# Attention and two MLPs in one kernel: scales packed with q and k, V loaded earlier, weight decodes held in program order

## The chip, the core and the metric

One core of a Trainium2 chip runs the kernel. TensorE multiplies matrices (PE in the rows; PEld is its loading of weights), VectorE (DVE) and ScalarE (ACT) work elementwise and can read TensorE's accumulators in PSUM, GpSimd (POOL) works elementwise on SBUF, and SyncE (SP) issues the DMAs between main memory and SBUF. Each engine takes its instructions in the order of its own list and waits on semaphores for the others. The metric is the device time of one execution in microseconds (us); less is better.

## The reference

Windowed attention over 4 sequences of 576 positions with 8 heads of 64, then a gated MLP, then a bilinear one. Everything is float32, apart from weights that arrive as 64-bit floats.

```python
scores = q @ k.T / 8 + slope[h] * -abs(i - j)   # masked outside 0 <= i - j < 128
x = softmax(scores) @ v                         # 2304 x 512 when heads are joined
h = x @ w_in                                    # 512 -> 2048
x = (s * relu(h) ** 2 + b) @ w_out              # 2048 -> 512
out = (((x @ w1) * (x @ w2)) @ w3) @ w_out2     # 512 -> 1024 -> 1024 -> 512
```

## The kernel before

The 2304 tokens go in six tiles of 384. Attention works by head: head number g counts through the tiles, 0 to 7 are tile 0's, 8 to 15 tile 1's. Tile 0's heads go as four pairs, in plain float32; from head 8 on operands are split into a high and a low part. A head has these steps: the scores `s` (TensorE, lines 292 or 297 and 298), the minimum with the bias `ns` (VectorE, line 311), a fold `pr` (VectorE, 320), the exponential (ScalarE, 328 or 334), the norm `sm` (VectorE, 344 and 345) and its product (GpSimd, 347), transposes `te` or `tp` (TensorE, 361 or 368), copies `oe` or `pp`, the masks `pt` (GpSimd, 384), and the product with V, `xo` or `pv` (TensorE, 401 or 421). For tile 0 a pair's result is divided by its sums on VectorE (`rs`, lines 433 and 436, and `xs`, 438), transposed (443) and copied by ScalarE to `xe` (461). Pairs are numbered 0 to 3. The four `xe` tiles are the input of tile 0's first MLP.

That MLP goes in 16 chunks of 128 hidden units, in plain float32: `hp` (TensorE, line 482) needs all four `xe` and one chunk of `w_in`; ScalarE takes relu and square; `acc` (534) needs them and one chunk of `w_out`. Later tiles use lines 491 and 540, three passes over split operands.

The 32 weight chunks arrive as 64-bit floats (`raw`), and each is **decoded** once: ScalarE reads the upper words (line 98, `z`), VectorE shifts (100), puts the sign in (103) and joins the lower words (109, `wz`). From tile 1 on a chunk must also be **split** into two parts: ScalarE makes the first (131), GpSimd or VectorE in turn the second (132). All chunks, decoded, raw and split, share one pool of 33 buffers, so that a split finds a free buffer only when the one before it, or the last decode, has given one back.

The program is written as `slot`s. Eight slots do tile 0's heads, with decodes ticked in between; then ten slots, in the order "BBBABBABBB", do one head of the next tile each, and in those with a B also two chunks of tile 0's MLP, with two decodes in the middle of the slot and one at its end. From the eighth MLP slot on, each does four splits. The order of the lists is not the written one: a list scheduler with its own idea of durations places each instruction on its engine when it thinks that the engine and the inputs are free, and so moves a ready instruction ahead of others. `keep_in_program_order` holds one instruction behind the instruction that was written just before it for the same engine:

```python
        if prev is not None:
            self.add_manual_dep(ins.ins, prev.name, ...)
```

Of the kernel before, what the change touches and what calls it, by code (L numbers as in the profile page):

```python
# [8 lines left out]
F32 = mybir.dt.float32  # L9
# [3 lines left out]
AF = mybir.ActivationFunctionType  # L13
ALU = mybir.AluOpType

B, H, S, D = 4, 8, 576, 64
# [5 lines left out]
P = 128  # L22
TT = 384
# [9 lines left out]
EARLY = H  # L33
# [4 lines left out]

@with_exitstack
def kernel(  # L40
    ctx: ExitStack, tc: tile.TileContext, qk0, qk, v, relm, w_in, w_out, s, b, w1, w2, w3T, wo2, qsc, v0, out
):
    nc = tc.nc
    PSUM = bass.MemoryType.PSUM

    const = ctx.enter_context(tc.tile_pool(name="const", bufs=1))
# [9 lines left out]
    ap = att_ctx.enter_context(tc.tile_pool(name="ap", bufs=1))  # L56

    zeros = ap.tile([P, DM], BF16, tag="xf", name="zeros")
    qsc_sb = const.tile([P, H // 2], F32, name="qsc_sb")
    relm_sb = const.tile([P, 4, 2 * P], F32, name="relm_sb")  # L60
    ident = const.tile([P, P], F32, name="ident")
    s_sb = const.tile([P, 1], F32, name="s_sb")
# [17 lines left out]
    def raw_load(dst, src):  # L80
        i = nc.sync.dma_start(out=dst, in_=src)
        if keep[0]:
            tc.keep_in_program_order(i)
        return dst

    def decode(raw, pool, tag, done, free=None, plain=False):

        z = zp.tile([P, DM], F32, tag="z", name="z")  # L90
        if raw.dtype == F32:
            nc.vector.tensor_copy(out=z, in_=raw)
            yield
        else:
            zu = z.bitcast(U32)
            wu = raw.bitcast(U32).rearrange("p (n t) -> p n t", t=2)
            wf = raw.bitcast(F32).rearrange("p (n t) -> p n t", t=2)
            nc.scalar.activation(out=z, in_=wf[:, :, 1], func=AF.Copy, scale=2.0 ** -112)
            yield
            nc.vector.tensor_scalar(  # L100
                out=zu, in0=zu, scalar1=3, scalar2=None, op0=ALU.logical_shift_left
            )
            nc.vector.scalar_tensor_tensor(  # L103
                out=zu, in0=wu[:, :, 1], scalar=0x80000000, in1=zu,
                op0=ALU.bitwise_and, op1=ALU.bitwise_or,
            )
            if plain:
                z = pool.tile([P, DM], F32, tag=tag, name="wz")
            nc.vector.scalar_tensor_tensor(
                out=z.bitcast(U32), in0=wu[:, :, 0], scalar=29, in1=zu,  # L110
                op0=ALU.logical_shift_right, op1=ALU.bitwise_or,
            )
            if plain:
                done(z)
                yield
                return
        if free:
            free()
        yield
        w = pool.tile([P, 2, DM], F32R, tag=tag, name="w")  # L120
        nc.scalar.activation(out=w[:, 0, :], in_=z, func=AF.Copy)
        nc.gpsimd.tensor_tensor(
            out=w[:, 1, :], in0=z, in1=w[:, 0, :].bitcast(F32), op=ALU.subtract
        )
        done(w)
        yield
# [53 lines left out]
    def pre_tick(more=True):  # L180
        for p in pres:
            if p[1] is None or next(p[1], p) is p:
                p[1] = None
                if more and npre[0] < len(late):
                    p[1] = predecode(npre[0], p[0])
                    npre[0] += 1
                    next(p[1])

    flight, todo, keep, raws, nraw, need = [], [], [True], [], [0], [0]

    def load_raws(n):
        for _ in range(n):
            if nraw[0] < len(raws):
                raw_load(*raws[nraw[0]])
                nraw[0] += 1
# [13 lines left out]
    qkraw, vraw, qa, ka, kb, vv, ns, pr, mins, sums, tps, pt, xf, xT, xo = ({} for _ in range(15))  # L209

    def att_load(g):
        if g < NG:
            if g < EARLY and g % 2:
                return
            raw = ap.tile([P, 2 * TT + P], F32, tag="qkraw", name="qkraw", bufs=2)
            nc.sync.dma_start(out=raw, in_=qk0[g // 2] if g < EARLY else qk[g - EARLY])
            if g < EARLY:
                qkraw[g + 1] = raw
            qkraw[g] = raw

    def att_load_v(g):
        if g < NG and g % 2 == 0:
            m = 2 * (D + 1) if g < EARLY else 2 * D
            raw = ap.tile([P, NB + 1, m], F32, tag="vraw", name="vraw", bufs=2)
            src = v0[g // 2] if g < EARLY else v[(g - EARLY) // 2]
            nc.sync.dma_start(out=raw.rearrange("p n d -> p (n d)"), in_=src)
            vraw[g // 2] = raw

    def att_split_q(g):
        if g < NG:  # L230
            sc = -0.125 * 2.0 ** (g % H + 1)
            q_r = qkraw[g][:, :TT]
            if g < EARLY:
                if g % 2 == 0:
                    p = g // 2
                    a = ap.tile([P, TT], F32, tag="qa", name="qe", bufs=2)
                    nc.scalar.activation(
                        out=a, in_=q_r, func=AF.Identity, scale=qsc_sb[:, p:p + 1]
                    )
                    qa[g] = qa[g + 1] = a  # L240
                return
            a = ap.tile([P, TT], F32R, tag="qa", name="qa", bufs=2)
            nc.scalar.activation(out=a, in_=q_r, func=AF.Copy, scale=sc)
            nc.vector.scalar_tensor_tensor(
                out=a[D:, :], in0=q_r[D:, :], scalar=sc, in1=a[D:, :].bitcast(F32),
                op0=ALU.mult, op1=ALU.subtract,
            )
            qa[g] = a

    def att_split_k(g):  # L250
        if g < NG:
            k_r = qkraw.pop(g)[:, TT:]
            if g < EARLY:
                ka[g] = k_r
                return
            k = ap.tile([P, TT + P], F32R, tag="ka", name="ka", bufs=2)
            kl = ap.tile([P, TT + P], F32R, tag="kb", name="kb", bufs=2)
            nc.scalar.activation(out=k, in_=k_r, func=AF.Copy)  # L258
            nc.gpsimd.tensor_tensor(  # L259
                out=kl, in0=k_r, in1=k.bitcast(F32), op=ALU.subtract  # L260
            )
            ka[g], kb[g] = k, kl
# [388 lines left out]
    for c in range(NC1):  # L651
        for d, src in ((wi, w_in[c]), (wo, w_out[c * P:(c + 1) * P, :])):
            raw = wp.tile([P, DM], src.dtype, tag="w", name="raw")
# [4 lines left out]
                )  # L658
            )
    att_load(0)  # L660
    warm = const.tile([P, 1], F32, name="warm")
    nc.gpsimd.memset(zeros, 0.0)
    nc.vector.memset(warm, 0.0)
    nc.scalar.activation(out=warm, in_=warm, func=AF.Exp)
    nc.sync.dma_start(out=qsc_sb, in_=qsc)
    nc.sync.dma_start(out=relm_sb[:, :2], in_=relm[:, :2])
    load_raws(4)
    att_load_v(0)
    att_load(2)
    nc.sync.dma_start(out=s_sb, in_=s)  # L670
    nc.sync.dma_start(out=b_sb, in_=b)
    make_identity(nc, ident)
# [90 lines left out]
        slot(n, None)  # L763
    flush(EARLY - 1)
    n, m = EARLY, 0
    for k in "BBBABBABBB":
        slot(n if k in "AB" else None, m if k in "MB" else None)
        n += k in "AB"
        m += k in "MB"
    assert (n, m) == (18, 8), (n, m)  # L770
    last = LEAD + (NTILE - 1) * NC1 // 2
    for n in range(n, last):
        if n == LEAD + NC1 - 1:
# [132 lines left out]
```

## Time and profile before

| what | us |
|---|---|
| median of three runs | 911.92 |
| lowest and highest of them | 906.9 and 913.98 |
| the profiled execution | 907.65 |
| its span, first to last instruction | 905.9 |
| TensorE busy in the span | 887.2 |
| VectorE, ScalarE, GpSimd busy | 484.6, 453.4, 340.4 |

The profiled execution lies 4.3 us under the median, within what the runs differ by. TensorE's busy time is that of its records, whose ends are modelled: where it is busy throughout with few instructions, it may still be waiting or running at half clock. So the table says where to look (TensorE), and a view by stretch of time says when it has too little to do.

### The profile page before, as it was taken

To read this page: it belongs to the slowest core of one execution; us is meant where nothing else is said; L and a number is where in the kernel's file an instruction comes from. 1 tells how busy PE (TensorE), PEld (TensorE's weight loads), DVE (VectorE), ACT (ScalarE), POOL (GpSimd) and SP (SyncE) were. 2 spreads that over 40 slices of the span, in tenths; PEclk is the share of its full clock that TensorE was granted. 3 is DMA by queue.
4 is the path that set the end of the run, shared out by engine and by line. 5 is a ranking of instruction groups with operands and counts; after the bars stand their busy time and mean duration, and the time that the engine had idled before them with its cause. 6 is when DMAs were issued, how large, how long until landed. Compare 5 with 4: busy or idle time off the path is not lost.

```text
span 905.9 us, 13384 instructions
## 1 busy us (share of the span) xinstructions
PE 887.2 (98%) x4833; PEld 805.5 (89%) x4836; DVE 484.6 (53%) x1012; ACT 453.4 (50%) x1052; POOL 340.4 (38%) x376
## 2 busy tenths in 40 slices
PE   8989989999999999999999999999999999999997
PEld 4756656999999999999999999899999999999996
DVE  5998866766688887788752621482211212121212
ACT  5756667776767787777754543342212121121211
POOL 0154687775567686777641301240101001010000
PEclk8989999999999999999999999999999999999999
DMA  8974211213334455445326962130201002000000
GB/s 312 304 283 166 100 64 46 85 59 112 99 127 166 169 201 170 145 157 181 117 94 224 385 261 84 56 116 1 71 1 35 36 1 70 1 36 1 35 1 36
DMA packets 37219, 104.38 MB, mean 115 GB/s; under 512 B 4512, under 2 KB 10656, under 8 KB 37152
## 3 DMA queue, kind: packets, MB, share of 16 engines
q1 hardware_dynamic: 37152, 103.52, 33.0%
q8 instruction: 38, 0.62, 0.3%
q14 instruction: 29, 0.24, 0.1%
HBM read 82.00 MB, written 21.50 MB: 114 GB/s over the span
## 4 chain that ended last, share of the span: by engine, by line
PE 85%; DVE 6%; issue 2%; POOL 2%; ACT 2%; DMA 2%; SPq 1%; DVEq 0%; ACTq 0%; POOLq 0%
PE ab L611 21%; PE acc L540 17%; PE hp L491 17%; PE acc L637 11%; PE hp L482 3%; PE acc L534 3%; PE pv L421 3%; PE w3a L575 2%; DVE z L103 2%; PE tp L368 1%; PE s L298 1%; PE s L297 1%; PE s L292 1%; DMA vraw<-v 1%; DVE z L100 1%
## 5 line engine op out<-in xcount | busy, mean ns | idle before, releaser
L611 PE MATMUL ab<-x,w 128*128 128x384 f32 x1152 | 208.3, 335 | 0.0
L611 PEld LDWEIGHTS ab<-x,w 128*128 128x128 f32 x1152 | 201.8, 188 | 4.3
L491 PE MATMUL hp<-x,w 128*128 128x384 f32 x960 | 186.2, 340 | 0.9 <-DVE pp L381 0.9
L540 PE MATMUL acc<-gh,w 128*128 128x384 f32 x640 | 177.3, 339 | 0.0
L491 PEld LDWEIGHTS hp<-x,w 128*128 128x128 f32 x960 | 167.6, 188 | 1.4 <-DVE pp L381 1.1
L625 DVE TENSOR_TENSOR a<-ab,a 128x384 f32<-128x384 f32 x48 | 26.7, 557 | 197.7 <-PE ab L611 179.8
L540 PEld LDWEIGHTS acc<-gh,w 128*128 128x128 f32 x640 | 115.3, 188 | 0.3
L540 PE MATMUL acc<-gl,w 128*128 128x384 f32 x320 | 108.6, 339 | 1.5 <-DVE gl L520 1.5
L599 POOL TENSOR_TENSOR x<-x,x 128x384 fp32r<-128x384 f32 x24 | 25.6, 1093 | 203.8 <-ACT x L598 191.9
L347 POOL TENSOR_SCALAR pr<-pr,sm 128x128 f32<-128x128 f32 x120 | 63.5, 543 | 88.3 <-DVE sm L345 34.7
L637 PE MATMUL acc<-w3o,ph 128*128 128x512 f32 x288 | 89.9, 394 | 0.0
L624 ACT ACTIVATE a<-ab 128x384 f32<-128x384 f32 x48 | 23.6, 492 | 131.7 <-PE ab L611 131.7
L259 POOL TENSOR_TENSOR kb<-qkraw,ka 128x512 fp32r<-128x512 f32 x40 | 56.2, 1404 | 71.4 <-ACT ka L258 71.3
L384 POOL TENSOR_SCALAR_AFFINE_SELECT pt<-pp 128x768 fp32r<-128x768 f32 x80 | 77.2, 986 | 7.0 <-PE pv L421 6.5
L520 DVE TENSOR_TENSOR gl<-r,gh 128x384 fp32r<-128x384 f32 x80 | 57.8, 723 | 33.6 <-ACT gh L512 32.4
L311 DVE CUSTOM_DVE_ANT_0 ns<-s,relm_sb 128x256 f32<-128x256 f32 (+1 forms) x144 | 52.9, 412 | 39.2 <-PE s L298 30.1
L626 ACT ACTIVATE ph<-a 128x384 fp32r<-128x384 f32 x48 | 25.2, 525 | 92.7 <-DVE a L625 92.7
L502 ACT ACTIVATE r<-hp 128x384 f32<-128x384 f32 x96 | 46.5, 486 | 49.6 <-PE hp L491 43.5
L540 PEld LDWEIGHTS acc<-gl,w 128*128 128x128 f32 x320 | 60.3, 188 | 2.3 <-DVE gl L520 2.2
L637 PEld LDWEIGHTS acc<-w3o,ph 128*128 128x128 f32 x288 | 53.4, 187 | 8.9
L637 PE MATMUL acc<-w3o,pl 128*128 128x512 f32 x144 | 56.5, 396 | 0.2 <-DVE pl L627 0.2
L334 ACT ACTIVATE pr<-pr,mn 128x128 f32<-128x128 f32 x120 | 46.8, 392 | 19.3 <-DVE pr L320 16.6
(89 smaller groups left out, 1423.4 us busy)
## 6 DMA issues: line engine op xcount, KB each, us to landing
qkraw<-qk SPq DMA_DIRECT2D x45, 448.0 KB, 3.3
late<-st SPq DMA_DIRECT2D x23, 512.0 KB, 3.4
w<-late SPq DMA_DIRECT2D x23, 512.0 KB, 7.1
raw<-w_in SPq DMA_DIRECT2D x16, 512.0 KB, 7.1
raw<-w_out SPq DMA_DIRECT2D x16, 512.0 KB, 6.7
raw<-w SPq DMA_DIRECT2D x16, 512.0 KB, 5.2
st<-w3T SPq DMA_DIRECT2D x15, 512.0 KB, 3.8
vraw<-v SPq DMA_DIRECT2D x20, 256.0 KB, 2.6
```

Of the source, the lines that this page charges most:

```text
L259: nc.gpsimd.tensor_tensor(out=kl, in0=k_r, in1=k.bitcast(F32), op=ALU.subtract)
L311: nc.vector.tensor_tensor_reduce(out=n[:, i, cs], in0=dst[i][:, cs], in1=relm_sb[:, VARIANT.get(t * NB + i, 0), cs], scale=2.0 ** -(h + 1) ...
L334: nc.scalar.activation(out=e[:, i, :], in_=e[:, i, :], func=AF.Exp, scale=-1.0, bias=mn[:, i:i + 1], accum_out=sm[:, i:i + 1],)
L347: nc.gpsimd.tensor_scalar(out=e[:, i, :], in0=e[:, i, :], scalar1=sm[:, i:i + 1], scalar2=1.0, op0=ALU.mult, op1=ALU.mult,)
L384: nc.gpsimd.affine_select(out=o[:, :, :, e, :], in_=pp.bitcast(F32), pattern=[[0, 2], [0, NB], [sign, P]], compare_op=op, fill=0.0, base=0 ...
L421: nc.tensor.matmul(out=d, lhsT=l, rhs=r, start=(n == 0), stop=(n == len(mms) - 1), skip_group_check=True)
L491: nc.tensor.matmul(out=hp, lhsT=wi[c][:, l, k * P:(k + 1) * P], rhs=xT[t, k][:, r, :], start=(n == 0), stop=(n == 3 * KD - 1),)
L502: nc.scalar.activation(out=rt[:, :TT], in_=hps.pop((t, c)), func=AF.Relu)
L520: nc.vector.tensor_tensor(out=gl, in0=rt[:, :TT], in1=gh.bitcast(F32), op=ALU.subtract)
L540: nc.tensor.matmul(out=x2acc[m], lhsT=wo[c][:, l, ms], rhs=g[r], start=(c == 0 and n == 0), stop=(c == NC1 - 1 and n == 2),)
L611: nc.tensor.matmul(out=d, lhsT=w[c][:, l, k * P:(k + 1) * P], rhs=x2[t, k][:, r, :], start=(n == 0), stop=(n == 3 * KD - 1),)
L637: nc.tensor.matmul(out=oacc[i], lhsT=p[l][:, cs], rhs=w3o[c][:, r, :], start=(c == 0 and n == 0), stop=(c == NC2 - 1 and n == 2),)
```

## The change

Three edits. The scale of each pair's q, which came by a DMA of its own (`qsc`, 16 bytes for each partition), is appended as a 897th column to the pair's q and k (`qk0`), and ScalarE reads it there. In the first loads, V of pair 0 now goes ahead of the weights, and the second pair's q and k stand after two weight chunks instead of four. In the ten slots of tile 0's MLP, three of a decode's four instructions (ScalarE's, and the first two of VectorE) are held in program order. Nothing else of the computation differs.

```diff
--- before.py
+++ after.py
@@ -38,7 +38,7 @@
-    ctx: ExitStack, tc: tile.TileContext, qk0, qk, v, relm, w_in, w_out, s, b, w1, w2, w3T, wo2, qsc, v0, out
+    ctx: ExitStack, tc: tile.TileContext, qk0, qk, v, relm, w_in, w_out, s, b, w1, w2, w3T, wo2, v0, out
...
-    qsc_sb = const.tile([P, H // 2], F32, name="qsc_sb")
...
@@ -88,6 +87,7 @@
         z = zp.tile([P, DM], F32, tag="z", name="z")
+        pin = tc.keep_in_program_order if pinned[0] else lambda i: i
...
@@ -95,15 +95,15 @@
-            nc.scalar.activation(out=z, in_=wf[:, :, 1], func=AF.Copy, scale=2.0 ** -112)
+            pin(nc.scalar.activation(out=z, in_=wf[:, :, 1], func=AF.Copy, scale=2.0 ** -112))
             yield
-            nc.vector.tensor_scalar(
+            pin(nc.vector.tensor_scalar(
                 out=zu, in0=zu, scalar1=3, scalar2=None, op0=ALU.logical_shift_left
-            )
-            nc.vector.scalar_tensor_tensor(
+            ))
+            pin(nc.vector.scalar_tensor_tensor(
                 out=zu, in0=wu[:, :, 1], scalar=0x80000000, in1=zu,
                 op0=ALU.bitwise_and, op1=ALU.bitwise_or,
-            )
+            ))
...
@@ -212,7 +213,8 @@
-            raw = ap.tile([P, 2 * TT + P], F32, tag="qkraw", name="qkraw", bufs=2)
+            n = 2 * TT + P + (1 if g < EARLY else 0)
+            raw = ap.tile([P, n], F32, tag="qkraw", name="qkraw", bufs=2)
...
@@ -232,10 +234,9 @@
-                        out=a, in_=q_r, func=AF.Identity, scale=qsc_sb[:, p:p + 1]
+                        out=a, in_=q_r, func=AF.Identity, scale=qkraw[g][:, -1:]
...
@@ -662,11 +663,11 @@
-    nc.sync.dma_start(out=qsc_sb, in_=qsc)
     nc.sync.dma_start(out=relm_sb[:, :2], in_=relm[:, :2])
-    load_raws(4)
     att_load_v(0)
+    load_raws(2)
     att_load(2)
+    load_raws(2)
...
@@ -763,11 +764,13 @@
     n, m = EARLY, 0
+    pinned[0] = True
     for k in "BBBABBABBB":
         slot(n if k in "AB" else None, m if k in "MB" else None)
         n += k in "AB"
         m += k in "MB"
     assert (n, m) == (18, 8), (n, m)
+    pinned[0] = False
```

The host side appends the scale to `qk0` and drops `qsc`.

How this moves the lists is shown at three places. SyncE's first issues before; `qkraw` is a pair's q and k, `relm` the bias table, `raw` a weight chunk, `vraw` a pair's V:

```order
L216 DMA qkraw<-qk 128x896
L665 DMA qsc_sb<-qsc 128x4
L666 DMA relm_sb<-relm 128x512
L81 DMA raw<-w_in 128x512
L81 DMA raw<-w_out 128x512
L81 DMA raw<-w_in 128x512
L81 DMA raw<-w_out 128x512
L226 DMA vraw<-v 128x520
L216 DMA qkraw<-qk 128x896
```

and with the change:

```order
L218 DMA qkraw<-qk 128x897
L666 DMA relm_sb<-relm 128x512
L228 DMA vraw<-v 128x520
L80 DMA raw<-w_in 128x512
L80 DMA raw<-w_out 128x512
L218 DMA qkraw<-qk 128x897
L80 DMA raw<-w_in 128x512
L80 DMA raw<-w_out 128x512
```

The small load is gone, V has moved from eighth to third, and the second pair's q and k from ninth to sixth.

VectorE's list before, from the sums of pair 3 (`rs`) to its output (`xs`); the rows of `z` and `wz` are decodes, those of `ns` the minimum of head 9:

```order
L433 TENSOR_SCALAR rs<-xo 128x6
L103 SCALAR_TENSOR_TENSOR z<-raw,z 128x512
L100 TENSOR_SCALAR z<-z 128x512
L436 RECIPROCAL rs<-rs 128x6
L109 SCALAR_TENSOR_TENSOR wz<-raw,z 128x512
L311 ISA ns,mn<-s_679,relm_sb 128x256
L311 ISA mn 128x1
L311 ISA ns,mn<-s_679,relm_sb 128x256
L311 ISA mn 128x1
L103 SCALAR_TENSOR_TENSOR z<-raw,z 128x512
L438 TENSOR_TENSOR xs<-xo,rs 128x384
```

and with the change, from pair 2's second `rs` row on; the first `xs` is pair 2's, the second pair 3's:

```order
L437 RECIPROCAL rs<-rs 128x6
L100 TENSOR_SCALAR z<-z 128x512
L439 TENSOR_TENSOR xs<-xo,rs 128x384
L103 SCALAR_TENSOR_TENSOR z<-raw,z 128x512
L245 SCALAR_TENSOR_TENSOR qa<-qkraw,qa 64x384
L109 SCALAR_TENSOR_TENSOR wz<-raw,z 128x512
L434 TENSOR_SCALAR rs<-xo 128x6
L437 RECIPROCAL rs<-rs 128x6
L439 TENSOR_TENSOR xs<-xo,rs 128x384
```

Pair 3's `rs`, reciprocal and `xs` now stand in one piece. Ahead of that `xs` VectorE has 12 whole decodes instead of 15, and the minima of heads 8 and 9, the fold of head 8 and head 9's `qa` have all moved behind it.

GpSimd's list before, around its first split (the row of `w`); the `pt` behind it is head 12's:

```order
L259 TENSOR_TENSOR kb<-qkraw,ka 128x512
L347 TENSOR_SCALAR pr<-pr,sm 128x128 x3
L132 TENSOR_TENSOR w<-wz,w 128x512
L384 AFFINE_SELECT pt<-pp 128x6x128 x2
L275 TENSOR_TENSOR vv<-vraw,vv 128x4x64 x2
L465 TENSOR_TENSOR x<-xf,x 128x384
```

and with the change, up to its first split; the `pt` ahead of it is head 15's:

```order
L276 TENSOR_TENSOR vv<-vraw,vv 128x4x64 x2
L466 TENSOR_TENSOR x<-xf,x 128x384
L260 TENSOR_TENSOR kb<-qkraw,ka 128x512
L348 TENSOR_SCALAR pr<-pr,sm 128x128 x3
L385 AFFINE_SELECT pt<-pp 128x6x128 x2
L132 TENSOR_TENSOR w<-wz,w 128x512
```

GpSimd's first split has moved behind three more heads. On ScalarE, 8 splits instead of 22 now stand ahead of the first relu of tile 1's MLP. TensorE's list keeps its order of stages; `hp` of chunks 3 and 4 moves behind `acc` of chunks 0 and 1. From head 24 on TensorE's list is the same.

## Rows read from the trace of the kernel before

**Rows 1.** Stretches: busy us (x count) of PE, PEld, DVE, ACT, POOL; PE clock; DMA.

```profile
0.00:36.00 36.00, 32.43 (x155) 20.79 (x157) 24.13 (x83) 23.25 (x51) 1.16 (x7) 0.91 0.86 295
...
40.00:61.00 21.00, 17.75 (x72) 11.16 (x72) 20.67 (x45) 13.58 (x37) 10.41 (x9) 0.84 0.86 311
...
61.00:90.00 29.00, 29.00 (x114) 18.61 (x112) 26.91 (x62) 17.50 (x40) 13.47 (x17) 1.00 0.55 193
...
90.00:110.00 20.00, 20.00 (x87) 13.42 (x86) 17.49 (x39) 12.56 (x33) 11.67 (x15) 1.00 0.33 113
...
110.00:126.00 16.00, 11.98 (x46) 7.58 (x46) 11.36 (x27) 10.69 (x29) 15.39 (x16) 0.89 0.13 46
...
126.00:160.00 34.00, 34.00 (x143) 22.75 (x142) 19.36 (x48) 24.42 (x57) 27.21 (x31) 1.00 0.18 57
```

**Rows 2.** The same view, where tile 1's MLP runs.

```profile
165.00:200.00 35.00, 35.00 (x219) 34.87 (x219) 22.49 (x51) 27.45 (x68) 25.15 (x30) 1.00 0.18 53
```

**Rows 3.** Timeline, 4 to 15 us: start, us, engine, line, out<-in, idle before and releaser.

```profile
4.34 0.61 ACT L237 ACTIVATE qe<-qkraw,qsc_sb 128x384 f32<-128x384 f32 x1 [2.04 <-DMA qsc_sb<-qsc]
...
8.24 0.66 ACT L98 ACTIVATE z<-raw 128x512 f32<-128x512 f32 x1 [3.29 <-DMA raw<-w_in]
...
12.85 1.96 PE L401 MATMUL xo<-vraw,oe 128*128 128x65 f32 x10 [1.32 <-DMA vraw<-v]
```

**Rows 4.** Timeline of VectorE: sums of pair 2, output of pair 3.

```profile
39.76 0.16 DVE L433 TENSOR_SCALAR rs<-xo 128x6 f32<-128x6 f32 x1
...
53.24 0.55 DVE L438 TENSOR_TENSOR xs<-xo,rs 128x384 f32<-128x384 f32 x1
```

**Rows 5.** The chain of waits: start, us, what.

```profile
54.98 4.21 PE hp L482 x6
...
110.27 1.24 POOL w L132
...
122.65 4.28 PE hp L482 x8
...
136.76 2.58 PE hp L482 x8
...
151.65 0.88 PE pv L421 x8
...
155.69 0.12 PE s L297
```

**Rows 6.** Timeline of TensorE, the last chunk of tile 0's MLP.

```profile
156.25 2.75 PE L534 MATMUL acc<-r,wz 128*128 128x386 f32 x8
```

**Rows 7.** VectorE's groups from 60 to 165 us: line, form, count, busy us, mean ns.

```profile
L109 DVE SCALAR_TENSOR_TENSOR wz<-raw,z 128x512 uint32<-128x512 uint32 x15 | 12.3, 820 | 0.1
...
L103 DVE SCALAR_TENSOR_TENSOR z<-raw,z 128x512 uint32<-128x512 uint32 x14 | 12.2, 875 | 0.2
...
L100 DVE TENSOR_SCALAR z<-z 128x512 uint32<-128x512 uint32 x14 | 6.7, 480 | 0.2
...
L311 DVE CUSTOM_DVE_ANT_0 ns<-s,relm_sb 128x256 f32<-128x256 f32 x27 | 10.1, 419 | 4.1 <-PE s L298 4.1
...
L244 DVE SCALAR_TENSOR_TENSOR qa<-qkraw,qa 64x384 fp32r<-64x384 f32 x9 | 9.5, 1055 | 0.8 <-ACT qa L243 0.5
...
L320 DVE TENSOR_TENSOR pr<-ns 128x384 f32<-128x384 f32 x9 | 7.2, 796 | 0.3
...
L344 DVE TENSOR_SCALAR sm<-sm 128x3 f32<-128x3 f32 x10 | 5.0, 498 | 1.3 <-ACT pr L334 1.3
...
L453 DVE TENSOR_TENSOR xf<-pv,cs 64x384 f32<-64x384 f32 x8 | 4.4, 549 | 3.7 <-ACT cs L452 3.7
...
L381 DVE TENSOR_TENSOR pp<-tp,pp 128x384 fp32r<-128x384 f32 x10 | 5.4, 545 | 2.2 <-ACT pp L380 2.2
```

**Rows 8.** VectorE's groups from 0 to 36 us.

```profile
L103 DVE SCALAR_TENSOR_TENSOR z<-raw,z 128x512 uint32<-128x512 uint32 x10 | 6.9, 687 | 0.1
```

**Rows 9.** Line 131, ScalarE's part of a weight's split: ns, first and last start.

```profile
L131 ACT ACTIVATE w<-wz x32: 612/630/636, 108.5 to 191.6; 128x512 fp32r<-128x512 f32 x32
```

More of the change, by code (lines that the diff above doesn't have):

```diff
@@ L187, in pre_tick @@
                     next(p[1])
+    pinned = [False]
     flight, todo, keep, raws, nraw, need = [], [], [True], [], [0], [0]
@@ L234, in att_split_q @@
                 if g % 2 == 0:
-                    p = g // 2
                     a = ap.tile([P, TT], F32, tag="qa", name="qe", bufs=2)
                     nc.scalar.activation(
-                        out=a, in_=q_r, func=AF.Identity, scale=qsc_sb[:, p:p + 1]
+                        out=a, in_=q_r, func=AF.Identity, scale=qkraw[g][:, -1:]
                     )
@@ L251, in att_split_k @@
         if g < NG:
-            k_r = qkraw.pop(g)[:, TT:]
+            k_r = qkraw.pop(g)[:, TT:2 * TT + P]
             if g < EARLY:
@@ L859 @@
         else:
-            qk0 = rows.reshape(H // 2, P, 2 * TT + P)
+            sc = (-0.125 * 2.0 ** (np.arange(H) + 1)).astype(np.float32)
+            sc = np.repeat(sc, D).reshape(H // 2, P, 1)
+            qk0 = np.concatenate([rows.reshape(H // 2, P, 2 * TT + P), sc], 2)
         vt.append(
@@ L889 @@
     arrays["wo2"] = inputs["moe2_w_out"]
-    sc = (-0.125 * 2.0 ** (np.arange(H) + 1)).astype(np.float32)
-    arrays["qsc"] = np.repeat(sc.reshape(H // 2, 2), D, 1).T
     arrays["v0"] = v0
```

## The prediction

> **What bounds the kernel now.** I read first the view by stretch, to see where TensorE has too little to do [rows 1]. From 61 to 110 us and from 126 to 160 it is busy throughout at the full clock of 2.4 GHz, and also where tile 1's MLP runs [rows 2]. Three stretches are left: the start (32.43 of 36 us busy), 40 to 61, and 110 to 126. The table says 887.2 busy of a span of 905.9, so nearly all that can be won without less work on TensorE lies ahead of 126 us, and an edit counts if it shortens one of these three or opens a new one.
>
> From 40 to 61 VectorE is busy 20.67 of 21 us [rows 1], TensorE 17.75. VectorE's timeline says why: pair 2's sums are worked on at 39.76, pair 3's output only at 53.24 [rows 4]; decodes and minima of heads 8 and 9 stand between them. The chain of waits shows what this holds: `hp` goes on at 54.98, in 4.21 us for six matmuls [rows 5], 0.70 each, where later eight take 2.58, 0.32 each. So TensorE waited, and just behind the wait runs at the lower clock, 1.2 GHz. The granted clock of that stretch, 0.84, gives 0.16 x 21 = 3.4 us lost to it.
>
> From 110 to 126 TensorE is busy 11.98 of 16 at a granted clock of 0.89 [rows 1]: 4.0 us idle and 0.11 x 16 = 1.8 to the clock. The chain of waits passes there through GpSimd's split at 110.27 (1.24 us), and `hp` at 122.65 takes 4.28 for eight [rows 5]: splits stand ahead of head 12's work on GpSimd, and the clock has fallen behind the wait again.
>
> **The start.** ScalarE's `qe` waits 2.04 us for the small load, and the first product with V waits 1.32 for V [rows 3]. Both look like gains. But the pair's q and k are in the same queue just ahead of the small load, so the wait changes its name; a small load's worth, some 0.2, is the most. V moved ahead puts the first weights later by its own size: 128 x 520 x 4 bytes = 266 KB at the stretch's 295 GB/s [rows 1] is 0.9 us. ScalarE's first decode row (8.24 us, waiting for its weight [rows 3]) stands ahead of head 0's exponentials, and what they hold is the copies that the same product needs beside V. So the 1.32 goes to that: at best 1.3 less, at worst 0.9 more. I take 0, since V and the weight trade places in one chain.
>
> **Pair 3's output.** In the new list VectorE has, behind pair 2's sums at 39.76 [rows 4], the reciprocal, one shift and pair 2's `xs`, all of them short: up to 41.0. Pair 2's transposes and heads 6 and 7's products follow on TensorE (20 records by 0.12 as `s` [rows 5] = 2.4, and hand-overs): 43.7. One half decode, one `qa` and one joining on VectorE lie beside these. Then pair 3's sums, reciprocal and `xs` in one piece, 45.2; and from `xs` to `hp` before took 54.98 - 53.24 = 1.74 [rows 4, 5], with the last of pair 3's products and hand-overs less: 46.5. So `hp` goes on 8.5 us earlier. TensorE's list has then done less: six matmuls of `hp` and the scores of head 9 are now behind, 6 x 0.32 + 6 x 0.12 = 2.7 us. Since the wait is short, I take the lower clock's 3.4 as won too. What is late next is `acc` of chunk 0: ScalarE has an exponential, two first steps of decodes (0.66 each [rows 3]), head 9's operands, relu and square ahead of it. I take 1.5, with 0 and 4 as ends.
>
> The sum goes by the end of tile 0's MLP, where TensorE's order is again the old one. It was 156.25 + 2.75 = 159.0 [rows 6]. From 54.98 that is 104.0, of which 3.4 + 4.0 + 1.8 were lost: 94.8 of work at full clock, with the 2.7 97.5. The new time without further waits is 46.5 + 1.5 + 97.5 = 145.5, **13.5 earlier**. In this the losses of 110 to 126 are taken as gone, because GpSimd's first split stands behind three more heads in the new list, as the order shows.
>
> **VectorE behind 46 us.** What left the path has to be done later: 12 whole decodes instead of 15 stand ahead of pair 3's `xs`, so 20 of 32 are left in place of 17. By VectorE's groups [rows 7] a decode is 0.480 + 0.875 + 0.820 = 2.18, and a head 3 x 0.419 + 1.055 + 0.796 + 0.498 + 0.549 + 0.545 = 4.70. So 20 x 2.18 + 10 x 4.70 = 90.5, beside TensorE's 97.5: 93%, as much as in 61 to 90 (26.91 of 29), where TensorE did not wait [rows 1]. But now the decodes stand at fixed places. In heads 11 and 14, whose slots have fewest chunks, TensorE's work between a head's scores and its transposes is two times 2.58 of `hp` or `acc`, a `pv` of 0.88 and 0.7 of scores [rows 5] = 6.8. On VectorE some 2.5 decodes (5.4) stand ahead of the minimum, which with the fold and the exponential's round trip (3 x 0.42 + 0.8 and as much again) makes about 8.3 for the one and, with half a decode more, 9.4 for the other. I take 1.5 + 2.6 = **4.1 of new waits**, with 0 and 9 as ends (none; both heads and two others, with a fallen clock each as it was at 122.65). The end of tile 0's MLP is then at 149.6.
>
> Line 103, the second step of a decode, takes 0.687 us where GpSimd is busy 1.16 of 36 us [rows 8, 1] and 0.875 in the stretch with GpSimd at work [rows 7]; the sum above uses the dearer one. The Trainium skill (SBUF — State Buffer, "Who interferes with whom") says that a VectorE instruction with two inputs in SBUF contends with a GpSimd one that reads SBUF, for it takes the same read interface; the two rows agree. The rule speaks against work moved beside GpSimd. If a decode's last two steps met GpSimd as it is from 126 to 160, busy 27.21 of 34 us with 0.88 an instruction [rows 1], and waited for half of one whenever it is busy, each would take 0.69 + 0.8 x 0.44 = 1.04, and 20 decodes 40 x 0.17 = 6.7 us more: 97.2 beside TensorE's 97.5, which leads to the second rival below. I keep the measured rows, as GpSimd's splits come late in the new list.
>
> **Splits.** 32 splits take ScalarE 0.63 each and run from 108.5 to 191.6 [rows 9]. ScalarE's new list has 8 instead of 22 ahead of tile 1's first relu; 24 remain beside tile 1's MLP, where 10 did before and TensorE was full while ScalarE was busy 27.45 of 35 and GpSimd 25.15 [rows 2]. Each 35 us then have 7.5 of ScalarE free, for 14 more by 0.63 = 8.8. The ends are 0 (all hidden, in the 80 us that tile 1's MLP lasts) and 24 x 0.63 = 15.1 (none). I take **2**, near the first, since the ten before cost nothing.
>
> The sum is -13.5 + 4.1 + 2 = -7.4 on the profiled 907.65: 900.3. The three timed runs and the profiled one have a mean of 910.1, 2.5 above the latter, so that the forecast is 903 beside the median of 911.92.
>
> **Rivals.** *No new wait*: VectorE keeps up as in 61 to 90 and the splits hide: -13.5, 894.2, and 897 with the 2.5. For it speaks the 93% with TensorE full; against it, that a list fixed in places can't fill a gap as the scheduler did. *VectorE sets the pace*: it did 28.85 of the 36 us from 90 to 126, 80%, where it wasn't ahead [rows 1]. At 80% its 90.5 us take 113, the MLP ends at 48 + 113 = 161, 2 later than before, with the splits' 2: +4, 911.7, or 914. The rule of the Trainium skill named above (SBUF — State Buffer) leads the same way. *Splits on the path*, the slower side: tile 1's `hp` and `acc` need their split weights and GpSimd's and ScalarE's part is in the list ahead of the relu of the same chunk; if none of the 24 finds a gap, -9.4 + 15.1 = +5.7, 913.3, or 916. It decides from the point where 15 of the 24 (9.4 / 0.63) are not hidden. *The change doesn't do what it says*: the joining step of a decode is held nowhere and the weights' arrival may let VectorE's list wait, so that `xs` is again late. Then only the start is left: 907 to 910.
>
> **How the numbers follow.** Some 1%, 9 us, is what a measurement of this kernel can tell from no change: the three runs before span 7. Chances: the forecast 0.47 (half of its spread of 898 to 908 is under 902.8, the limit of 1%), no new wait 0.18, VectorE's pace 0.20, splits 0.10, no effect 0.05. Faster: 0.24 + 0.18 and a little off for the last's edge = 0.41. Slower than 921: a fifth of the pace's and of the splits' cases, 0.06. The rest, 0.53, is within 1%. A range of 893 to 915 leaves out half of the splits' case and the far ends of the next two.
>
> **What the changed profile would show.** Right: pair 3's `xs` at about 45, `hp` going on at 46 to 47 and no granted clock under 1.00 behind it; no wait at 119 to 122; the end of `acc` of chunk 15 at about 150; TensorE's waits in heads 11 and 14, ended by VectorE; line 131 from some 130 to 230, with TensorE busy throughout. The start should show the first product with V waiting for ScalarE's copies in place of V. The prediction is wrong on the fast side if VectorE's list has slack in heads 11 and 14; on the slow side if `acc` of chunk 0 waits far over 4 us, if decodes wait for weights with minima queued behind them, or if TensorE has gaps of a split's length in tile 1's MLP.

## The result

The changed kernel takes 898.46 us (median of 22 runs) beside 906.83 of the kernel before (22 runs with it); the ratio is 0.9907, with a 95% interval from 0.9887 to 0.9926. It is faster, by 8.4 us. The forecast of 903 beside 911.92 was a ratio of 0.990, so the size was met; but the largest chance, 0.53, stood on "within 1%", and a measurement that knows the ratio to 0.2% doesn't call this no change. The terms of the sum were not all right either. The profiled execution took 898.25 us, with a span of 896.5 (905.9 before).

### The profile page after: what moved, and what is told of

It is laid out like the page before. It is cut to its first block, busy times and chain, and to the rows that moved or that the text cites. A ratio compares the mean times of both kernels' runs of the same rounds, so it can differ in the third digit from the quotient of the medians.

```text
span 896.5 us, 13371 instructions
## 1 busy us (share of the span) xinstructions
PE 882.4 (98%) x4833; PEld 803.5 (90%) x4836; DVE 492.4 (55%) x1012; ACT 450.1 (50%) x1052; POOL 348.7 (39%) x376
## 4 chain that ended last, share of the span: by engine, by line
PE 83%; DVE 8%; ACT 3%; issue 2%; DMA 2%; POOL 2%; SPq 0%; DVEq 0%; POOLq 0%; ACTq 0%
PE ab L612 21%; PE acc L541 17%; PE hp L492 17%; PE acc L638 11%; PE pv L422 3%; PE acc L535 2%; PE hp L483 2%; PE w3a L576 2%; DVE z L103 2%; PE s L298 1%; PE s L299 1%; PE tp L369 1%; DVE z L100 1%; DMA raw<-w_in 1%; PE s L293 1%
## 5 line engine op out<-in xcount | busy, mean ns | idle before, releaser
L385 POOL TENSOR_SCALAR_AFFINE_SELECT pt<-pp 128x768 fp32r<-128x768 f32 x80 | 79.5, 1015 | 18.5 <-DVE pp L382 8.2
L312 DVE CUSTOM_DVE_ANT_0 ns<-s,relm_sb 128x256 f32<-128x256 f32 (+1 forms) x144 | 52.6, 412 | 27.3 <-PE s L299 20.4
```

What stands on the lines that cost most here:

```text
L312: nc.vector.tensor_tensor_reduce(out=n[:, i, cs], in0=dst[i][:, cs], in1=relm_sb[:, VARIANT.get(t * NB + i, 0), cs], scale=2.0 ** -(h + 1) ...
L385: nc.gpsimd.affine_select(out=o[:, :, :, e, :], in_=pp.bitcast(F32), pattern=[[0, 2], [0, NB], [sign, P]], compare_op=op, fill=0.0, base=0 ...
```

## The profile after

The view by stretch of the changed kernel, with the columns of [rows 1]:

```profile
0.00:36.00 36.00, 33.50 (x189) 22.19 (x193) 26.75 (x92) 25.84 (x58) 1.16 (x7) 1.00 0.88 331
36.00:61.00 25.00, 24.51 (x105) 16.12 (x104) 21.21 (x48) 16.14 (x40) 14.59 (x14) 1.00 0.78 281
61.00:90.00 29.00, 28.69 (x121) 18.96 (x120) 23.89 (x56) 17.08 (x45) 17.90 (x21) 1.00 0.39 133
90.00:110.00 20.00, 18.65 (x82) 12.47 (x80) 17.18 (x39) 11.64 (x31) 13.50 (x14) 1.00 0.52 186
110.00:126.00 16.00, 15.14 (x59) 9.66 (x60) 15.28 (x33) 10.76 (x28) 11.72 (x14) 1.00 0.25 85
150.00:160.00 10.00, 7.49 (x39) 7.35 (x38) 8.48 (x19) 8.11 (x17) 7.00 (x9) 0.83 0.31 105
```

Against [rows 1 and 2]: the start has the full clock throughout (0.91 before), 40 to 61 too, and 110 to 126 has lost 0.9 us where it lost 5.8. New are small gaps at 61 to 110, which was full, and a large one at 150 to 160: 2.5 us idle and 0.17 x 10 = 1.7 at the lower clock.

Two marks on TensorE's timeline, the first `hp` of tile 0's MLP and the last `acc` of it, divide the span into three parts. Before, the scores of heads 2 and 3 and the first `hp`:

```profile
14.80 2.50 PE L292 MATMUL s<-qkraw,qe 64*128 64x128 f32 x6
...
20.11 1.35 PE L292 MATMUL s<-qkraw,qe 64*128 64x128 f32 x6
...
40.49 1.46 PE L482 MATMUL hp<-xe,wz 128*128 128x384 f32 x4
```

After, on the timeline of all engines: ScalarE's first decode step, the first product with V, and the scores of heads 2 and 3; head 2's take 1.35 us in place of 2.50:

```profile
7.89 0.66 ACT L98 ACTIVATE z<-raw 128x512 f32<-128x512 f32 x1 [3.26 <-DMA raw<-w_in]
...
10.93 1.33 PE L402 MATMUL xo<-vraw,oe 128*128 128x65 f32 x10
...
12.19 1.35 PE L293 MATMUL s<-qkraw,qe 64*128 64x128 f32 x6
...
14.99 1.35 PE L293 MATMUL s<-qkraw,qe 64*128 64x128 f32 x6
```

On TensorE's timeline after, the first `hp` and the one behind pair 3's transposes:

```profile
36.32 1.46 PE L483 MATMUL hp<-xe,wz 128*128 128x384 f32 x4
...
44.38 3.82 PE L483 MATMUL hp<-xe,wz 128*128 128x384 f32 x11 [0.42 <-DVE mn L312]
```

The same view where the MLP ends and tile 1's begins:

```profile
143.63 2.79 PE L535 MATMUL acc<-r,wz 128*128 128x386 f32 x8
...
153.78 2.58 PE L492 MATMUL hp<-x,w 128*128 128x384 f32 x9 [2.51 <-DVE pp L382]
```

The lower clock of the start before is seen in its row of 12 to 20 us:

```profile
12.00:20.00 8.00, 6.93 (x24) 4.91 (x25) 6.63 (x17) 4.67 (x11) 0.00 (x0) 0.58 0.93 350
```

The changed kernel has 1.00 there. The first `hp` has moved from 40.49 to 36.32: **4.2 us won in the start**, where the prediction had 0. The MLP's end has moved from 159.0 [rows 6] to 143.63 + 2.79 = 146.4, by 12.6: so **8.4 won between**, where the prediction had 9.4. The span has shrunk by 9.4: **3.2 given back** behind, where it had 2. So it is 4.2 + 8.4 - 3.2 = 9.4, against 0 + 9.4 - 2 = 7.4. The 4.2 are made up as follows. The first product with V begins 1.9 us earlier (10.93 against 12.85 [rows 3]). From there to head 3's scores the same matmuls take 4.06 us in place of 7.26, so 3.2 are the clock (0.42 x 8 = 3.4 by the granted clock of 12 to 20). From head 3's scores to the first `hp` it is 21.3 in place of 20.4, 0.9 given back.

Pair 3's output, on VectorE's timeline, to be read against [rows 4]:

```profile
40.74 0.56 DVE L439 TENSOR_TENSOR xs<-xo,rs 128x384 f32<-128x384 f32 x1
```

Its `xs` starts at 40.74 in place of 53.24. The `hp` behind it comes at 44.38 since TensorE had scores and eight matmuls ahead of it; the only wait there is 0.42 us, for a minimum of VectorE.

TensorE's longest line in the view of waits, 61 to 126 us (total, times, longest):

```profile
PE tp L369 <- POOL pr L348: 2.0, 2, 1.7
```

And its only one from 126 to 165:

```profile
PE hp L492 <- DVE pp L382: 2.5, 1, 2.5
```

The longer of the two for `tp` is at 110.82, head 14, the other at 80.89, head 11. Line 131, against [rows 9]:

```profile
L131 ACT ACTIVATE w<-wz x32: 613/632/636, 135.0 to 224.2; 128x512 fp32r<-128x512 f32 x32
```

## The experiments

All ratios are to the kernel before. Twelve kernels were run.

**Pins alone** and **the start alone**: the diff cut in two.

```diff
 pins alone (on the kernel before)
...
+            pin(nc.scalar.activation(out=z, ...))
...
+            pin(nc.vector.tensor_scalar(...))
+            pin(nc.vector.scalar_tensor_tensor(...))
...
+    pinned[0] = True
     for k in "BBBABBABBB":
 the start alone (on the changed kernel)
-    pinned[0] = True
```

> The kernel before with the three decode steps held in program order in the ten slots, and its old start (small load kept, V behind four weights). Theory 1, the terms add: TensorE's losses behind the start shrink by about 8.5 us, 3 come back where tile 1's MLP begins, so 5.4 us faster than before (ratio 0.994), with the lower clock still there at 13 to 20 us. Theory 2, what was predicted: the start is worth nothing, the pins all of it: 8 to 9 us faster (0.990). Theory 3, the pins only work with the earlier start: within 1 us of before.

> The changed kernel with nothing held in program order: both start edits alone. Theory 1, the terms add: 4.0 us faster than before (0.9956), pair 3's output late again as VectorE has the same queue ahead of it, TensorE waiting and at the lower clock behind that. Theory 2, as predicted: within 1 us of before (0.999 to 1.001). Theory 3: more than 6 us faster, since an earlier start moves the scheduler's whole list.

Pins alone give 0.9952 (0.9918 to 0.9986; 903.3 us), the start alone 0.9952 (0.9929 to 0.9975; 903.5). The product is 0.9904, the whole change 0.9907: by the times the halves add, as Theory 1 had it, and what was predicted (all from the pins, none from the start) is refuted. Their traces show where. With the start alone, by stretch:

```profile
36.00:61.00 25.00, 23.15 (x99) 14.89 (x98) 24.62 (x56) 17.17 (x42) 12.07 (x11) 1.00 0.83 294
61.00:110.00 49.00, 45.14 (x186) 29.16 (x184) 44.04 (x100) 30.26 (x74) 30.21 (x33) 1.00 0.42 139
110.00:126.00 16.00, 12.53 (x49) 8.29 (x50) 10.30 (x23) 10.68 (x29) 14.80 (x18) 0.89 0.25 74
```

Pair 3's output isn't late there: its `xs` starts at 43.50, with no pin at all, and TensorE keeps the full clock up to 110 us. This part of Theory 1's expectation failed. But 3.9 us are idle from 61 to 110, and 110 to 126 still loses 3.5 + 1.8. The splits begin at 104.6 there, and GpSimd does one of them (1.28 us, at 113.91) ahead of the masks and `pr` for which TensorE waits 2.7. With the pins alone, in an execution of 907.43 us:

```profile
20.00:32.00 12.00, 12.00 (x41) 8.40 (x41) 6.16 (x22) 5.02 (x12) 0.00 (x0) 0.50 0.72 238
110.00:126.00 16.00, 13.83 (x54) 8.93 (x52) 14.55 (x36) 10.00 (x27) 9.68 (x11) 0.89 0.35 109
```

The lower clock stays until 32 us, behind the same wait for V as before (1.33) and one of 0.57 for ScalarE's `qe`; 110 to 126 still loses 2.2 + 1.8. The two marks on TensorE's timeline, with the start alone:

```profile
36.46 1.46 PE L483 MATMUL hp<-xe,wz 128*128 128x384 f32 x4
...
151.97 2.75 PE L535 MATMUL acc<-r,wz 128*128 128x386 f32 x8
```

and with the pins alone:

```profile
46.38 1.46 PE L484 MATMUL hp<-xe,wz 128*128 128x384 f32 x4
...
155.47 2.76 PE L536 MATMUL acc<-r,wz 128*128 128x386 f32 x8
```

Between the marks lie 118.3 us with the start alone, 111.9 with the pins alone, 118.5 before and 110.1 in the changed kernel. So the start's gain is ahead of the first `hp` (4.0), and of the 8.4 behind it the pins alone win 6.7 and the start alone 0.3; the rest comes only with both. Pair 3's output is another matter: its `xs` is 12.8 us behind the first `hp` before, 7.0 with the start alone, 6.4 with the pins alone and 4.4 with both. With the start alone this advance is spent in the waits from 61 to 126.

**The start's two edits apart**: only the scale with q and k; only the order of the loads.

```diff
 scale only (on the kernel before)
-    nc.sync.dma_start(out=qsc_sb, in_=qsc)
...
+                        out=a, in_=q_r, func=AF.Identity, scale=qkraw[g][:, -1:]
...
 V first only (on the kernel before)
-    load_raws(4)
     att_load_v(0)
+    load_raws(2)
     att_load(2)
+    load_raws(2)
```

> The kernel before with only the scale appended to q and k. Theory 1: the bias table lands 1.0 to 1.2 us earlier (some 4.7 in place of 5.83) and the first minima start 0.9 earlier, but the first product with V still waits for V, so that the lower clock behind it stays: 1.0 us faster (0.999). Theory 2, as predicted: 0.2 us at most, since the small load's wait changes its name. Theory 3, the small load is the whole of the start's gain: 4 us faster (0.9956).

> The kernel before with only the new order of the loads: V ahead of the weights, the second pair's q and k behind two of them; the small load stays. Theory 1: the wait of 1.32 us for V is gone, with it the lower clock at 13 to 20 us (3.4 us), and the weights come 0.6 later: 2.5 to 3.5 us faster (0.9965). Theory 2, as predicted: 0, since the product waits for ScalarE's copies instead, which the later weight holds up. Theory 3: the wait is gone but the clock falls all the same: 1 us faster.

The scale alone gives 0.9992 (0.9961 to 1.0023), the order alone 1.0014 (0.9971 to 1.0056): neither can be told from nothing, though together they give 0.9952. For the scale Theory 1's "1.0 faster" (0.999) and the predicted 0.2 can't be told apart by the time. The ten times with V first lie far apart: three are 903.2 to 904.1, where the start alone lies (902.0 to 905.6), with a granted clock of 0.995 or 0.996 over the execution, and five are 912.1 to 914.5, with 0.984 to 0.986. So what the order alone is worth can't be read from these ten times. The trace is of one of the five (913.14 us); ScalarE's first decode step, head 0's transposes, and the product with V:

```profile
9.25 0.66 ACT L98 ACTIVATE z<-raw 128x512 f32<-128x512 f32 x1 [4.14 <-DMA raw<-w_in]
...
10.34 1.15 PE L361 MATMUL te<-ident,ns 128*128 128x128 f32 x5 [1.41 <-ACT ns L328]
...
12.53 2.23 PE L401 MATMUL xo<-vraw,oe 128*128 128x65 f32 x10
```

The first weight comes 1.0 us later than before (9.25 against 8.24 [rows 3]; the two other traces with the old loads have 7.58 and 8.59), head 0's exponentials stand behind its decode step on ScalarE, and TensorE waits 1.41 for them in place of 1.32 for V. That is the trade that the prediction named, and Theory 2 was right about it. The granted clock from 12 to 32 us is then 0.50. In the changed kernel the weight comes at 7.89, and in the seven others here that have both edits at 7.92 to 8.40, and neither wait is left. That the missing small load does this rests on one trace with V first, and with the scale alone the weight is at 8.11, no earlier than the old loads can have it. With the scale alone, the product still waits for V, on TensorE's timeline:

```profile
12.65 1.99 PE L400 MATMUL xo<-vraw,oe 128*128 128x65 f32 x10 [1.27 <-DMA vraw<-v]
```

**V behind the first weight**, with the small load kept:

```diff
-    load_raws(4)
+    load_raws(1)
     att_load_v(0)
+    load_raws(1)
     att_load(2)
+    load_raws(2)
```

> The kernel before, scale's small load kept, with V behind the first weight and ahead of the second, and the second pair's q and k behind two weights. Theory 1: V alone ahead of all weights gained nothing because the first weight then came 1 us later and head 0's exponentials, which stand behind its decode step on ScalarE, with it (a wait of 1.41 us, and the lower clock as before). Here the first weight lands as before (about 8.2 us) and V about 9, so that neither wait is there and the granted clock stays at 1.00: 3 to 4.5 us faster (0.995 to 0.997), the same as both start edits. Theory 2: the small load's 1 us in the queue is itself needed: within 1.5 us of before.

0.9971 (0.9949 to 0.9993). The weight's step starts at 7.63, the product with V waits 0.46 for ScalarE's copies, and the clock is full:

```profile
7.63 0.68 ACT L98 ACTIVATE z<-raw 128x512 f32<-128x512 f32 x1 [2.81 <-DMA raw<-w_in]
...
11.55 1.33 PE L401 MATMUL xo<-vraw,oe 128*128 128x65 f32 x10 [0.46 <-ACT oe L375]
```

The view by stretch:

```profile
12.00:20.00 8.00, 7.78 (x50) 5.61 (x50) 7.44 (x25) 6.74 (x16) 0.00 (x0) 1.00 0.99 360
```

The gain of 2.6 us lies below the 3 to 4.5 of Theory 1 and above the 1.5 of Theory 2, with an interval that holds both; the trace is Theory 1's, its first `hp` at 36.65 beside the changed kernel's 36.32. So the small load needn't go: it is enough that neither V nor the first weight is late.

**The wait filled**: matmuls with zeros, 6 more, in the wait for V. Their results are overwritten.

```diff
-            keep_active(s0..., 2 if g else 10)
+            keep_active(s0..., {0: 10, 2: 8}.get(g, 2))
```

> The kernel before with one thing changed: six more of the matmuls with zeros stand on TensorE ahead of head 2's scores, 0.22 us each, so that TensorE works through the 1.3 us in which the first product waits for V; loads, scale and list are the old ones. Their results are overwritten. Theory 1, the start's gain is TensorE's clock and the clock falls behind the idle time: granted clock 1.00 from 13 to 20 us though V comes as late as before, 3 to 4 us faster (0.996). Theory 2, the gain comes from V and the bias table landing earlier: within 1 us of before, lower clock as before.

0.9978 (0.9947 to 1.0010), between the two theories. In the profiled execution TensorE ran at half its pace from its start on, ahead of the wait; its timeline, with the scores of head 1, the eight matmuls with zeros, the first product with V, head 3's scores and the first `hp`:

```profile
9.15 2.50 PE L292 MATMUL s<-qkraw,qe 64*128 64x128 f32 x6
...
13.48 2.15 PE L75 MATMUL s<-zeros 128*128 128x512 bf16 x8
15.47 1.23 PE L401 MATMUL xo<-vraw,oe 128*128 128x65 f32 x10
...
19.42 1.35 PE L292 MATMUL s<-qkraw,qe 64*128 64x128 f32 x6
...
39.80 1.46 PE L482 MATMUL hp<-xe,wz 128*128 128x384 f32 x4
```

The view by stretch there:

```profile
6.00:13.40 7.40, 7.40 (x21) 4.42 (x22) 4.54 (x17) 3.40 (x8) 0.00 (x0) 1.00 0.97 352
12.00:20.00 8.00, 8.00 (x44) 5.62 (x43) 6.90 (x19) 5.44 (x14) 0.00 (x0) 1.00 0.94 360
```

Behind the filled wait the clock stays full, and from the product with V to head 3's scores it is 3.95 us in place of 7.26: 3.3 won by the clock alone, with the old loads and the old list. From there to the first `hp` it is 20.38 us in both. The product itself begins 2.6 later than before (15.47 against 12.85), behind a first stretch at half pace, so that only 0.7 is left at the first `hp`. So Theory 1 is right about the clock, and the time lies between the theories because of that late product, as far as this one execution shows.

**The fourth step held too.**

```diff
-            nc.vector.scalar_tensor_tensor(   # line 109
+            pin(nc.vector.scalar_tensor_tensor(
...
```

> The changed kernel with the fourth step of a decode (line 109) held in program order too. Theory 1, VectorE has little slack and each thing held costs waits in heads whose slots are short: 1 to 4 us slower than the changed kernel (0.992 to 0.995 of before). Theory 2, the free fourth step changes nothing, since it is always behind the third: the same as the changed kernel, 0.990 to 0.991.

0.9914 (0.9882 to 0.9946), 898.7 us: as the changed kernel, so the rival that the free fourth step undoes the change has no ground, and holding it costs nothing. Theory 2.

**Pins in the first three slots only.**

```diff
         n += k in "AB"
         m += k in "MB"
+        pinned[0] = m < 3
```

> The changed kernel with decodes held only in the first three of the ten slots. Theory 1, the gain is pair 3's output alone and the later pins cost the waits at 80 to 110 us (4.3 us in the changed kernel): these waits go, but the splits again come ahead of heads 12 to 15 (15 instead of 9 on ScalarE's list ahead of tile 1's first rounding) and cost some of the 5.8 us that they cost before: 0.988 to 0.993. Theory 2, the later pins are what keeps the splits back and is worth the most: 4 us or more slower than the changed kernel (0.995 or above).

1.000 (0.9964 to 1.0035). Theory 2: 8 us of the changed kernel's gain are lost though the start and pair 3's output (`hp` at 44.41) are as there. By stretch:

```profile
90.00:110.00 20.00, 18.09 (x74) 11.81 (x73) 19.64 (x45) 11.67 (x26) 11.72 (x13) 0.97 0.58 209
110.00:126.00 16.00, 12.74 (x47) 7.80 (x46) 13.39 (x30) 10.31 (x28) 9.24 (x14) 0.93 0.17 58
```

Here the splits start at 121.6, and still 3.3 us are idle and the clock is 0.93 from 110 to 126. The long wait, on TensorE's timeline, ends ahead of the first split:

```profile
117.55 0.33 PE L369 MATMUL tp<-ident,pr 128*128 128x128 f32 x1 [3.06 <-POOL pr L348]
```

GpSimd's masks ahead of `pr` wait 3.9 us for VectorE's `pp`, and the rows ahead of that `pp` are decodes and steps of a head. So this stall is not the splits'. The later pins are needed.

**Splits from the fifth slot on.**

```diff
-            split_some(4 if m >= 7 else 0)
+            split_some(4 if m >= 4 else 0)
```

> The changed kernel with the splits allowed from the fifth MLP slot on in place of the eighth: seven splits stand ahead of the last decode on ScalarE. Theory 1, the loss of 4.5 us at 150 to 157 comes from splits beside the end of tile 0's MLP, and earlier splits spread it: 1 to 3 us faster than the changed kernel (0.988 to 0.990). Theory 2, splits earlier bring back the stall of heads 12 and 13 as before: 3 to 6 us slower than the changed kernel (0.994 to 0.997).

0.9977 (0.9943 to 1.0011): Theory 2. With splits from 105.6 on, 110 to 126 is worse than before, 4.1 us idle at a clock of 0.79:

```profile
110.00:126.00 16.00, 11.93 (x36) 7.36 (x37) 11.32 (x24) 9.46 (x26) 9.35 (x14) 0.79 0.35 117
```

**Who makes the second step of a split.** All on VectorE, all on GpSimd, and the first eight on GpSimd with the rest by turns.

```diff
-            weight_split(*unsplit.pop(0), nc.vector if e % 2 else nc.gpsimd)
+            weight_split(*unsplit.pop(0), nc.vector)        # all on VectorE
+            weight_split(*unsplit.pop(0), nc.gpsimd)        # all on GpSimd
+            nsplit[0] += 1                                  # first eight on GpSimd
+            late_v = e % 2 and nsplit[0] > 8
+            weight_split(*unsplit.pop(0), nc.vector if late_v else nc.gpsimd)
```

> The changed kernel with the second step of all 32 splits on VectorE in place of every other one on GpSimd. Theory 1: the loss of 4.5 us at 150 to 157 is VectorE's small steps held up by GpSimd's splits (sm took 1.27 us beside one, 0.17 otherwise): that loss halves, 2 us faster than the changed kernel (0.9885). Theory 2: it is the length of VectorE's and ScalarE's queues: 16 more splits by 0.69 make it 1 to 4 us slower (0.992 to 0.995).

> The changed kernel with the second step of all 32 splits on GpSimd. Theory 1 (VectorE held up by GpSimd's splits): more of them, so 2 to 5 us slower than the changed kernel (0.993 to 0.996). Theory 2 (the length of VectorE's queue): VectorE has 11 us less to do, so 1 to 2 us faster (0.9885 to 0.9895).

> The changed kernel with the second step of the first eight splits on GpSimd alone, the others by turns as before. Theory 1: the loss of 4.5 us where tile 1's MLP begins is VectorE's queue, in which four splits stand ahead of head 16's copies; with these on GpSimd it falls to about 1 us, as with all splits there, and since the others go by turns GpSimd does not become the bound later (7 us were lost at 185 to 210 with all on it): 3 us faster than the changed kernel (0.987). Theory 2: GpSimd's queue is late already with eight, and head 16 and 17 wait for it instead: the same as the changed kernel or up to 3 us slower (0.991 to 0.994).

0.9925 (0.9899 to 0.9952; four runs only), 1.0038 (1.0004 to 1.0072) and 0.9926 (0.9899 to 0.9952). None beats the changed kernel. Where the wait goes is seen by stretch, first with all on GpSimd:

```profile
150.00:160.00 10.00, 9.58 (x61) 9.34 (x60) 5.67 (x16) 7.81 (x18) 9.26 (x11) 1.00 0.34 113
165.00:200.00 35.00, 32.76 (x198) 31.23 (x198) 21.82 (x43) 24.99 (x62) 32.97 (x35) 1.00 0.20 65
```

With the first eight on GpSimd:

```profile
126.00:150.00 24.00, 23.05 (x98) 15.57 (x97) 17.78 (x41) 14.61 (x38) 15.51 (x18) 1.00 0.12 41
150.00:160.00 10.00, 9.09 (x56) 8.51 (x55) 5.64 (x18) 7.69 (x21) 9.26 (x11) 1.00 0.42 146
200.00:240.00 40.00, 38.80 (x243) 37.95 (x242) 30.33 (x64) 30.72 (x79) 30.38 (x34) 1.00 0.27 89
```

With all on GpSimd the gap at 150 to 160 is nearly gone (0.4 us idle, full clock, against 2.5 and 0.83), and the wait for VectorE's `pp` with it. But GpSimd is then busy 32.97 of 35 us and TensorE waits for the split weights themselves, as the view of waits from 150 to 240 us shows:

```profile
PE hp L492 <- ACT w L131: 7.0, 3, 3.1
```

That is 12 us over the changed kernel, slower than either theory had it. With the first eight on GpSimd, 0.9 idle is left at 150 to 160, 0.95 comes ahead of it and 1.2 behind 200: the gap has moved, not gone, and the time is Theory 2's. All on VectorE is Theory 2's by its time too, though the interval also holds the changed kernel's; in its trace the wait for `pp` is gone as well, `sm` takes 0.16 us, and 1.7 us are idle at 150 to 160, in a wait for ScalarE's `r`. So the wait for `pp` goes with the splits on one engine, whichever it is. That the length of VectorE's queue alone made it isn't shown. The work has no other place where it costs nothing.

## Why the prediction was near in size and wrong in its parts

The step that failed is **the start**: "I take 0, since V and the weight trade places in one chain." It was 4.2: 1.9 from the product with V, 3.2 from the clock, 0.9 given back. The trade is real, as the trace with V first alone shows, and the scale alone is worth nothing that shows either. What was wrong was to take the same for both together: there the weight landed at 7.9 behind V, in place of 9.2 with V first alone, and neither wait was left. V behind the first weight shows the same with the small load kept: the two need not trade places at all. The sign named for it, the product with V waiting for ScalarE's copies, didn't come: its row at 10.93 has no wait. And what carried the larger part was never priced: of 0 to 36 the busy time was quoted and not the granted clock of 0.91 [rows 1], though 0.42 x 8 = 3.4 us of the lower clock stood between 12 and 20, behind the wait for V. The prediction counted this price at both later stalls and forgot it at the first.

The second failure is in the chances. "Some 1%, 9 us, is what a measurement of this kernel can tell" was taken from three runs that span 7; 22 runs give 0.2%. The forecast stood 0.2 us from the edge of 1%, and half of its chance was called no change for that. That the ratio came within 0.001 is luck in part. In the trace the sum was 2.0 short, -7.4 for -9.4, since the missing 4.2 of the start met 1.0 and 1.2 too much behind it. And 903 was built on the mean of 910.1 and then set beside the median of 911.92, which made 8.9 of the 7.4. The median of 22 is 5 lower than that of three.

**Pair 3's output** went as predicted: `xs` at 40.74 where 45.2 less the start's 4.2 is 41.0, no granted clock under 1.00 from there to 126. The 1.5 us taken for a late `acc` of chunk 0 didn't come: 0.5 us are idle in all from 36 to 61. That the pins do it was only half right: the start alone brings `xs` forward as well, but wins next to nothing by it up to the MLP's end (0.3).

**VectorE behind it**: predicted were waits in heads 11 and 14 of 1.5 + 2.6; they came in these two heads, as 0.3 and 1.7, and TensorE was idle 2.5 us in all from 61 to 126 (0.31 + 1.35 + 0.86). The releaser was not VectorE but GpSimd's `pr`, one step on: in head 14 VectorE's `pp` comes late, GpSimd's two masks wait for it, and `pr` stands behind them:

```profile
108.71 1.69 POOL L385 TENSOR_SCALAR_AFFINE_SELECT pt<-pp 128x768 fp32r<-128x768 f32 x2 [2.33 <-DVE pp L382]
110.39 1.07 POOL L348 TENSOR_SCALAR pr<-pr,sm 128x128 f32<-128x128 f32 x3
```

The rows for a decode were a little cheap: 2.18 us for each was used, and the 20 from 46 to 146 us took 0.60 + 0.87 + 0.92 = 2.39.

**The stall of heads 12 and 13** is gone as predicted, 0.9 us lost in place of 5.8. That it needs the splits to be behind is shown by the run that changes nothing else: with splits from the fifth slot (their start at 105.6) it is back. That this is not enough is shown by the pins in three slots: TensorE waits 3.1 us there before the first split, behind a late `pp` of VectorE. So the term was about right in size, and named one of its two conditions. How much of the stall with the start alone is the splits' stays open: the one split in front of the masks takes 1.28 us, and the wait is 2.7.

**The splits** run from 135.0 to 224.2 (predicted 130 to 230), and the 2 us for them were 3.2. The mechanism was not among those named, and the clock, said to be full all the way, fell to 0.83 behind it. TensorE didn't wait for split weights but, once, for VectorE's copies `pp` of a head; its queue held splits, tile 0's last steps and `sm` ahead of them. The 2.5 + 1.7 lost there are more than the 3.2; where the other 1.0 is won back stays open. The slower rival (TensorE waiting for the split weights) is what all on GpSimd shows: 1.0038.

## What to carry to other kernels

Where one step needs two loads, an edit that brings one forward can hold the other back; price the order as a whole, by asking what is late next. Here V ahead of all weights exchanged a wait of 1.32 us for one of 1.41, and V behind the first weight left 0.46. A short wait in front of TensorE is to be priced with the granted clock of the stretch behind it, in every place where it occurs, also in the first microseconds. Before one trace stands for a kernel, its time and clock are to be held against those of the other executions: with V first alone they went from 903 to 914.5 us. Where work is held back to free a stage, the stage that gets it needs free time on all engines that share it: moving the splits between VectorE and GpSimd moved the wait and won nothing.

## What the runs showed of the hardware

Behind a wait of 1.3 us the lower clock lasted about 6.7 us in one execution (the kernel before, 0.42 x 8 us at half clock) and all of 20 to 32 in another (pins alone, 0.50, TensorE busy 12.00 of 12), where a second wait of 0.57 us stood 1.9 us behind the first. In the run with the filled wait TensorE took 2.50 us for six scores that take 1.35 at full speed, at a granted clock of 1.00 in that stretch: ahead of the first stretch at full pace the granted clock didn't show the half pace there.

A load of 2 KB in all, 16 bytes for each partition, cost the load behind it far more than its bytes: the bias table of 256 KB landed at 5.6 to 6.2 us in the five traces that have the small load, and at 4.6 to 5.3 in the nine without it. Some 0.5 of this is the issue, at 1.71 in place of 1.24 us on SyncE. The first minimum, which needs that table, gained nothing from it in the kernel with the scale alone (6.93 against 7.04), since it waits for TensorE's scores there.

A VectorE instruction that takes 0.17 us in the median of its 40 (`sm`, 128 x 3) took 1.27 us when it started together with a split of GpSimd; their rows on the timeline of the changed kernel:

```profile
151.34 1.26 POOL L132 TENSOR_TENSOR w<-wz,w 128x512 fp32r<-128x512 f32 x1 [1.29 <-ACT w L131]
151.36 1.27 DVE L345 TENSOR_SCALAR sm<-sm 128x3 f32<-128x3 f32 x1
```

The Trainium skill (SBUF — State Buffer, "Who interferes with whom") says that such an instruction of VectorE can take the pair of ports that it shares with GpSimd, and that whoever comes second waits for the whole of the other's instruction; GpSimd's began 0.02 us ahead, and the row agrees. It stands in VectorE's queue ahead of the `pp` that TensorE waits for at 150 to 160, and lengthens that queue by 1.1 us.
